# Sparse attention and gated convolution on one core: another division of the DMA issues, fp32 bounds for six pairs, and the order planned again

## The chip, the cores and the metric

The kernel runs on one core of a Trainium2 chip. Five engines work side by side, each through its own list of instructions in order: TensorE (PE in the rows), VectorE (DVE), ScalarE (ACT), GpSimd (POOL) and SyncE (SP), which here only issues DMAs. The metric is the device time of one execution in microseconds; the median of several runs is compared.

## The reference

For 4 batches of 8 heads (768 rows, head size 64) each query may look at 6 of the 24 chunks of 32 keys. Chunks are chosen by an upper bound of the score:

```
k_min, k_max = min and max of k over each chunk
ub   = sum(max(q * k_min, q * k_max)) over the head dimension   # causal chunks only
top  = the 6 chunks with the largest ub
attn = softmax(0.125 * q @ k.T, masked to top and causal)
x    = attn @ v, heads side by side                             # [4, 768, 512]
gate = sigmoid(causal depthwise conv of x, 5 taps)
out  = (gate * (x @ w_val)) @ w_out
```

## The kernel before

The work is cut into 16 pairs of heads, four to a batch. For a pair p the kernel issues small operations, named as the planner names them (name, pair, part):

- **Lk, Lq, Lv** load k, q and v from memory (line 914 for k and q, two DMAs each, line 910 for v) into three buffers of each kind. **KT, QT** transpose k and q on TensorE (line 923), **KE, QH** evict them on ScalarE as fp16 (lines 930 and 966), and **KX** takes the chunk maxima and minima on VectorE (line 936).
- **KB** (lines 946 to 961) and **QL, RL, RH** (lines 974 to 985) split the bounds' operands into a high and a low fp16 part, and **BD** (line 1002) forms the upper bounds with 30 matmuls of 48 columns.
- **MB, T8, CM** (lines 1005 to 1019) add the causal fill `cfill`, take the largest eight and make the mask NS. **MD** (line 1034) transposes NS into QM by DMA; for the pairs not in the set `dmam` **MT and ME** do it on TensorE and VectorE.
- **S** (lines 1046 to 1051) makes the scores in six blocks of two PSUM banks each, the mask being one more matmul of QM with the constant EM. **E** (line 1055) takes the exponential on ScalarE, **A** (line 1067) cuts the causal triangle on GpSimd, and **AV, RC, NR** (lines 1076 to 1087) sum the values and normalize into ON.
- **XT** (line 1105) transposes ON into xT by DMA for the pairs in `dmat`, and **XS** (lines 1111 and 1114) copies halves of it. **CV** (lines 1149 to 1155) is the convolution as 40 matmuls on a quarter of the array each, **TH** (line 1159) its gate on ScalarE.
- When the four pairs of a batch are done, **VL** (line 1166) multiplies by w_val, **GV** gates it on VectorE, **OU** (line 1179) multiplies by w_out, **OE** evicts and **ST** (line 1193) stores.

The order is not written by hand. `schedule` is a list planner: it knows each operation's cost on its engine, picks the ready operation with the lowest priority number that can start soonest, and hands out the eight PSUM banks. The priorities come from the table PARAMS (a period per pair, an offset per kind, an offset per kind and pair). The instructions are then emitted in the planned order, and each engine keeps to it. The planner counts a DMA that ScalarE issues as 100 ns of ScalarE, and one that SyncE issues as 60 ns of SyncE.

Constants (`ident`, `cfill`, `identh`, EM, `ident2`, the convolution weights) are loaded on SyncE's queue between the first loads (lines 1207 to 1227); w_val and w_out on GpSimd's. DMAs from SyncE and ScalarE use eight completion semaphores in turn, so that the ninth waits for the first to land.

Of the kernel before, what the change touches and what calls it, by code (L numbers as in the profile page):

```python
# [10 lines left out]
FP = mybir.dt.float32  # L11
# [63 lines left out]
MODE = 90.0  # L75
XLAT = {"PE": 37, "ACT": 60, "DVE": 57, "POOL": 60, "SP": 60}


def schedule(graph, nbanks=8, quota=None, slack=0.0):
# [15 lines left out]
    dma_free = [0.0, 0.0]  # L95
# [3 lines left out]
    while len(order) < n:  # L99
        best = None  # L100
        for e in engs:
# [5 lines left out]
            tried = 0  # L107
            for pri, i in sorted(r):
# [9 lines left out]
                new = [g for g in o.groups if g.bank is None]  # L118
                if new:
# [5 lines left out]
                    av = sorted(bank_free[b] for b in range(nbanks) if not bank_open[b])  # L125
                    if len(av) < len(new):
                        continue
                    if av[len(new) - 1] > est:
                        est = av[len(new) - 1]
                if cand is None or est < cand[0] - slack:  # L130
                    cand = (est, pri, i)
# [5 lines left out]
            if cand is not None and (best is None or cand < best):  # L137
# [3 lines left out]
        est, pri, i = best  # L141
# [3 lines left out]
        for g in o.groups:  # L145
            if g.bank is None:
                b = min((bank_free[b], b) for b in range(nbanks) if not bank_open[b])[1]
# [4 lines left out]
        if o.dma:  # L152
            q = o.eng == "ACT"
            dma_free[q] = max(dma_free[q], est + 700.0) + o.dma * (1.5 if q else 1.0)
            o.fin = dma_free[q] + 1300.0
            if q:
                dma_free[0] += o.dma
# [15 lines left out]
        for sidx in o.succs:  # L173
# [14 lines left out]
PARAMS = {'T': 11966.2,  # L188
 'off': {'Lk': -41636,
         'Lq': -33293,  # L190
         'Lv': 48651,
         'Lw': -20469,
         'Lc': -37356,
         'Ld': 61141,
         'KT': -17145,
         'KE': -135276,
         'KX': -10835,
         'KB': -27580,
         'QT': -12221,
         'QH': -36726,  # L200
         'QL': -53332,
         'RH': -896,
         'RL': -6554,
         'VC': 15582,
         'BD': -13273,
         'MB': -57904,
         'T8': -43761,
         'CM': -237738,
         'MT': -84078,
         'ME': -110955,  # L210
         'S': -3769,
         'E': 380,
         'A': 4500,
         'AV': 5996,
         'NR': 7483,
         'XT': 29413,
         'XS': 129182,
         'XE': 31813,
         'CV': 28979,
         'TH': 93088,  # L220
         'VL': 38301,
         'VLz': -27255,
         'GV': 27368,
         'OU': 65453,
         'OUz': -23813},
 'kbeng': ['POOL', 'POOL', 'POOL'],
 'border': [5, 4, 3, 1, 0, 2],
 'sstep': 1157.8,
 'avA': 10953.2,
 'avB': 13593.9,  # L230
 'vstep': 2846.9,
 'ostep': 613.2,
 'dmat': {3, 4, 5, 6, 7, 8, 9, 10, 11, 12, 13, 14, 15},
 'dmam': {4, 5, 6, 7, 8, 10, 12, 13, 14},
 'xeng': {'XT': 'DVE', 'XS': 'ACT'},
 'cvcost': 1650.0,
 'quota': {'s': 8, 'av': 2, 'w': 8},
 'slack': 100.0,
 'dl': {('VC', 1): 9000,
        ('RH', 4): -1736,  # L240
        ('Lv', 14): -6295,
        ('OUz', 4): 378,
        ('TH', 13): -13394,
        ('XE', 0): -5226,
        ('E', 14): -4155,
        ('KT', 4): -16168,
        ('TH', 1): 32754,
        ('KT', 6): -1203,
        ('XS', 7): 10081,
        ('KE', 8): -46,  # L250
        ('MT', 14): -14186,
        ('RH', 3): -5716,
        ('E', 4): -17454,
        ('T8', 2): 10374,
        ('Lc', 3): 5791,
        ('RH', 6): -1437,
        ('CM', 2): 15061,
        ('QT', 2): 7714,
        ('CM', 7): -6969,
        ('NR', 3): -2699,  # L260
        ('QT', 5): -214,
        ('KE', 4): 14340,
        ('CV', 4): -2772,
        ('ME', 10): 731,
        ('NR', 4): 3599,
        ('QH', 14): -8614,
        ('VC', 13): -2339,
        ('KX', 13): 578,
        ('XT', 10): -3543,
        ('OUz', 13): -7327,  # L270
        ('VL', 8): -982,
        ('T8', 13): 11117,
        ('KB', 5): -383,
        ('XE', 14): 10692,
        ('MT', 11): -2513,
        ('E', 2): 635,
        ('QL', 3): -3942,
        ('RH', 1): -6652,
        ('RL', 9): 685,
        ('AV', 13): -2326,  # L280
        ('KE', 0): 4923,
        ('AV', 2): -1335,
        ('RH', 2): -954,
        ('VLz', 12): 5318,
        ('CV', 9): -10708,
        ('KT', 9): 46,
        ('Ld', 3): 3582,
        ('S', 14): -5473,
        ('MB', 2): -20083,
        ('KB', 4): 7639,  # L290
        ('T8', 9): 1891,
        ('KB', 2): 2873,
        ('MT', 13): -11694,
        ('VL', 3): -357,
        ('Lw', 8): -483,
        ('QT', 0): -1113,
        ('GV', 13): 2356,
        ('Lk', 14): 22746,
        ('Lq', 15): -20461,
        ('QT', 11): -349,  # L300
        ('OU', 6): -1209,
        ('Lk', 13): -7175,
        ('RH', 0): 20291,
        ('AV', 4): -632,
        ('QL', 1): 18148,
        ('Lk', 10): -568,
        ('KX', 5): -403,
        ('A', 4): 6402,
        ('OU', 14): 5538,
        ('S', 6): -408,  # L310
        ('E', 1): -921,
        ('Lw', 14): 21861,
        ('XE', 10): 3312,
        ('BD', 13): 1202,
        ('A', 13): -3892,
        ('Ld', 13): 19053,
        ('KT', 3): -2737,
        ('KE', 2): 32991,
# [992 lines left out]
```

## Time and profile before

| | us |
|---|---|
| median of 3 runs | 223.14 (222.56 to 225.15) |
| the profiled execution, its own time | 221.15 |
| its span, first to last instruction | 219.4 |
| TensorE busy in the span | 187.2 (85%) |
| VectorE, ScalarE, GpSimd busy | 142.3, 141.4, 95.3 |

Busy time leaves out instructions that issue DMAs. A TensorE record lasts until the modelled end of its matmul, so a row of matmuls overlaps itself.

### The profile page before, as it was taken

The page shows a single profiled execution, that of the slowest core. Times are in us where ns is not written, and L with a number is a line of the kernel's source. Part 1 is how long each engine was busy: PE and PEld are TensorE (multiplying, and loading weights), DVE is VectorE, ACT ScalarE, POOL GpSimd, SP SyncE. Part 2 cuts the span into 40 slices and gives each one's busy share as a digit, 9 for nine tenths or more (in the row PEclk, how much of TensorE's full clock was granted, in tenths as well). Part 3 has the DMA queues.
Part 4 walks back from the last instruction along what each step waited for, and adds up shares of the span by engine and source line. Part 5 has one row for each costly group of instructions (what it writes and reads, how often), then busy time and mean ns, then how long its engine had stood idle before and what let it go on. Part 6 is the DMA issues. An engine that isn't in the chain of part 4 may idle for free.

```text
span 219.4 us, 7282 instructions
## 1 busy us (share of the span) xinstructions
PE 187.2 (85%) x2854; PEld 122.2 (56%) x2854; DVE 142.3 (65%) x458; ACT 141.4 (64%) x313; POOL 95.3 (43%) x237
## 2 busy tenths in 40 slices
PE   1147878989899878898999996989998999999992
PEld 1025555757767555565564683556565666765540
DVE  0419988599885988575671798857576488252332
ACT  3013667979778866686696942877977686925241
POOL 6206499977456635351613521553723633500000
PEclk9999699999999999999999999999999999999998
DMA  5999999983996999439939999901347150139035
GB/s 99 197 198 231 220 201 224 213 186 76 185 211 126 235 169 198 92 71 152 153 105 208 288 187 222 127 23 40 27 143 231 24 69 18 39 57 292 22 118 217
DMA packets 98893, 32.32 MB, mean 147 GB/s; under 512 B 92796, under 2 KB 95788, under 8 KB 98860
## 3 DMA queue, kind: packets, MB, share of 16 engines
q1 hardware_dynamic: 79276, 25.50, 56.1%
q10 hardware_dynamic: 18528, 5.32, 16.5%
q0 software_dynamic: 1056, 1.05, 3.1%
q8 instruction: 22, 0.36, 0.7%
q14 instruction: 11, 0.09, 0.2%
HBM read 21.30 MB, written 6.29 MB: 126 GB/s over the span
## 4 chain that ended last, share of the span: by engine, by line
PE 54%; DVE 15%; DMA 10%; ACT 8%; SPq 4%; issue 3%; POOL 2%; ACTq 2%; DVEq 0%
PE ps L1179 10%; PE ps L1166 7%; PE ps L1149 7%; PE ps L1076 6%; PE ps L1048 5%; PE ps L923 5%; ACT P L1055 5%; PE ps L1051 5%; PE ps L1002 4%; DMA QM<-NS 3%; DMA identh<-identh 3%; SPq L914 3%; PE ps L1151 3%; DVE KK L936 2%; DMA xS<-xT 2%
## 5 line engine op out<-in xcount | busy, mean ns | idle before, releaser
L1055 ACT ACTIVATE P<-ps 128x512 f16<-128x512 f32 (+1 forms) x192 | 89.8, 575 | 18.2 <-PE ps L1051 13.1
L1067 POOL TENSOR_SCALAR_AFFINE_SELECT P<-P 128x128 f16<-128x128 f16 (+1 forms) x128 | 48.3, 393 | 39.7 <-ACT P L1055 37.3
L936 DVE TENSOR_REDUCE KK<-ps 128x12 f32<-128x384 f32 x64 | 32.7, 550 | 13.0 <-ACT KE L930 8.3
L1051 PE MATMUL ps<-QM,EM 64*128 64x512 f16 (+4 forms) x256 | 37.9, 295 | 1.5 <-DVE QM L1032 0.8
L1048 PE MATMUL ps<-QH,KE 64*128 64x512 f16 (+4 forms) x256 | 35.3, 297 | 1.0 <-ACT OSB L1187 0.4
L1151 PE MATMUL ps<-xS,diag 64*64 64x384 f16 x160 | 29.0, 324 | 2.3 <-DVE ON L1087 1.6
L1149 PE MATMUL ps<-xT,diag 64*64 64x384 f16 x160 | 29.4, 325 | 0.0
L1076 PE MATMUL ps<-VA,P 128*128 128x65 f16 x672 | 27.6, 194 | 1.9 <-POOL P L1067 1.1
L1076 PEld LDWEIGHTS <-P 128*128 128x128 f16 x672 | 25.1, 98 | 7.4 <-issue 3.5
L1153 PE MATMUL ps<-xS,diag 64*64 64x384 f16 x160 | 29.0, 325 | 0.0
L1155 PE MATMUL ps<-xT,diag 64*64 64x384 f16 x160 | 29.0, 325 | 0.0
L1159 ACT ACTIVATE G<-ps 128x384 f32<-128x384 f32 x32 | 14.9, 508 | 20.3 <-PE ps L1155 14.3
L974 DVE SCALAR_TENSOR_TENSOR QL<-ps,QH 128x256 f16<-128x256 f32 (+1 forms) x32 | 15.0, 487 | 18.2 <-ACT QH L966 18.0
L1171 DVE SCALAR_TENSOR_TENSOR GV<-G,ps 128x384 f16<-128x384 f32 x32 | 17.4, 548 | 13.8 <-ACT G L1159 7.5
L1166 PE MATMUL ps<-xT,wval 128*128 128x384 f16 x128 | 24.6, 326 | 0.7 <-ACT G L1159 0.5
L989 POOL CAST VA<-vn 128x768 f16<-128x768 f32 x16 | 13.5, 850 | 23.2 <-PE ps L1076 21.7
L966 ACT ACTIVATE QH<-ps 128x384 f16<-128x384 f32 x32 | 15.1, 508 | 12.1 <-PE ps L923 10.3
L923 PE MATMUL ps<-ident,qn 128*128 128x128 f32 x96 | 16.5, 302 | 7.5 <-DMA qn<-in_q_dram 7.3
L1179 PE MATMUL ps<-wout,GV 128*128 128x512 f16 x96 | 22.4, 379 | 0.0
L930 ACT ACTIVATE KE<-ps 128x384 f16<-128x384 f32 x32 | 15.3, 520 | 10.7 <-PE ps L923 7.8
L923 PE MATMUL ps<-ident,kn 128*128 128x128 f32 x96 | 15.7, 298 | 7.3 <-DMA kn<-in_k_dram 5.2
L1149 PEld LDWEIGHTS <-diag 64*64 64x64 f16 x160 | 15.8, 106 | 9.4 <-issue 4.7
(58 smaller groups left out, 365.6 us busy)
## 6 DMA issues: line engine op xcount, KB each, us to landing
vn<-in_v_dram SPq DMA_DIRECT2D x16, 384.0 KB, 5.8
out_dram<-OSB SPq DMA_DIRECT2D x24, 256.0 KB, 2.7
kn<-in_k_dram SPq DMA_DIRECT2D x30, 192.0 KB, 4.6
qn<-in_q_dram SPq DMA_DIRECT2D x30, 192.0 KB, 4.5
xS<-xT ACTq DMA_DIRECT2D x13, 48.5 KB, 2.2
xS<-xT ACTq DMA_DIRECT2D x13, 48.0 KB, 2.7
wval<-in_moe_w_val_dram POOLq DMA_DIRECT2D x1, 512.0 KB, 6.9
wout<-in_moe_w_out_dram POOLq DMA_DIRECT2D x1, 512.0 KB, 9.3
```

Of the source, the lines that this page charges most:

```text
L923: nc.tensor.transpose(out=pt[:, tl * 128:(tl + 1) * 128], in_=t[:, 3 * w + tl, :], identity=ident)
L936: nc.vector.tensor_reduce(out=KK[p % 2][:, mx, w * 12:(w + 1) * 12], in_=bank(gr, None).rearrange("p (c t) -> p c t", t=CH), axis=AX.X, op ...
L1048: nc.tensor.matmul(out=pq[hh][:, col + a:col + n], lhsT=KE[p % 3][HP[hh], ks], rhs=QH[p % 3][HP[hh], q0 + a:q0 + n], start=True, stop=False)
L1051: nc.tensor.matmul(out=pq[hh][:, col + a:col + n], lhsT=EM[HP[hh], ks], rhs=qm[HP[hh], q0 + a - 128:q0 + n - 128], start=False, stop=True)
L1055: e.EX = lambda p, hh, bi, tot, gr: nc.scalar.activation(out=PT[hh, bi, p % 2][:, 0:tot], in_=bank(gr, None)[:, 0:tot], func=AF.Exp, scale ...
L1067: nc.gpsimd.affine_select(out=ap, in_=ap, pattern=[[0, n], [1, 128]], compare_op=ALU.is_ge, fill=0.0, base=0, channel_multiplier=-1)
L1076: nc.tensor.matmul(out=pav[:, qt, :], lhsT=PT[a, bi, p % 2][:, col:col + 128], rhs=VA[p % 3][:, hh, jt, :], start=(jt == 0), stop=(jt == qt))
L1149: nc.tensor.matmul(out=b0[0:64], lhsT=diag[0:64, ct, 0, j, :], rhs=x[0:64, LD - 4 + ki:LD - 4 + ki + HB], start=st, stop=sp)
L1151: nc.tensor.matmul(out=b1[0:64], lhsT=diag[64:128, ct, 0, j, :], rhs=xs[64:128, a:a + HB], start=st, stop=sp)
L1153: nc.tensor.matmul(out=b0[64:128], lhsT=diag[0:64, ct, 1, j, :], rhs=xs[0:64, LD - 4 + ki:LD - 4 + ki + HB], start=st, stop=sp)
L1166: nc.tensor.matmul(out=pv, lhsT=wval_sb[:, ct, et * 128:(et + 1) * 128], rhs=xT[:, s0 + ct, LD + w * HB:LD + (w + 1) * HB], start=(ct == 0 ...
L1179: nc.tensor.matmul(out=po, lhsT=GVT[(b % 2) * NCT + et][:, s * 128:(s + 1) * 128], rhs=wout_sb[:, et, :], start=(et == 0), stop=(et == NCT ...
```

## The change

- The DMA transposes MD and XT and the copies XS go from ScalarE's queue to SyncE's. The first load of q and `ident` go to ScalarE's queue; all other constants go to GpSimd's.
- For the pairs 0, 1, 2, 3, 5 and 11 (`f32`) the bounds are formed in fp32. QL, RL, RH, KB and BD fall away. In their place ScalarE evicts q and relu(q) as fp32 (QF and RF, two pieces each, line 1088), VectorE makes four small tiles KF (lines 1075 and 1077), and BF takes 10 fp32 matmuls of 48 columns (line 1096).
- For the last batch a value sum VL may be split: the first three of its four matmuls as soon as their pairs are transposed, the fourth when the last pair is.
- The planner gets other costs (1240 ns of SyncE for a transpose, 480 for a copy, 800 for a load of k or q), one line of DMA time for all queues, a rule that holds a DMA back while more than 4 us are queued, and a rule that keeps banks for an operation that needs two. PARAMS is new throughout: the score blocks come in the order 3, 0, 1, 4, 2, 5, only one AV bank is open at a time, and the sets are `dmat` = 1 and 4 to 15, `dmam` = 5 to 15.

```diff
+DEEP = 4000.0
+AHEAD = 1000.0
...
+                if o.dma and dma_free - DEEP > est:
+                    est = dma_free - DEEP
...
+                    take = av[held:held + len(new)]
+                    if len(take) < len(new):
+                        if est <= f + AHEAD:
+                            held += len(new)
                         continue
...
-            q = o.eng == "ACT"
-            dma_free[q] = max(dma_free[q], est + 700.0) + o.dma * (1.5 if q else 1.0)
+            dma_free = max(dma_free, est + 700.0) + o.dma
...
- 'border': [5, 4, 3, 1, 0, 2],
+ 'border': [3, 0, 1, 4, 2, 5],
- 'quota': {'s': 8, 'av': 2, 'w': 8},
+ 'quota': {'s': 6, 'av': 1, 'w': 8, 'v': 2},
+ 'lq': {('q', 0): 'ACT'},
+ 'f32': {0, 1, 2, 3, 5, 11},
...
+            if full:
+                g.op("ACT", c, l, f"QF{p}.{w}", lambda w=w, gr=gr: e.QFv(p, w, gr, 0),
+                     [("qps", p, w)], [("QF", k2, w)], [gr], pri(p, "QL", w))
...
+                g.op("PE", 2 * 112, 112 + 285, f"BF{p}.{it}", lambda it=it, gr=gr: e.BF(p, it, gr),
...
-            g.op("ACT", 100, 100, f"MD{p}", lambda: e.MD(p), [("NS", k2)], [("QM", k3)], (),
+            g.op("SP", 1240, 1240, f"MD{p}", lambda: e.MD(p), [("NS", k2)], [("QM", k3)], (),
                  pri(p, "MT"), dma=1050.0)
...
-            g.op("ACT", 100, 100, f"XT{p}", lambda: e.XTd(p), on, [("xT", slot)], (), pri(p, "XT"),
+            g.op("SP", 1240, 1240, f"XT{p}", lambda: e.XTd(p), on, [("xT", slot)], (), pri(p, "XT"),
...
+                    cuts = ((0, NCT),) if not last else ((0, NCT - 1), (NCT - 1, NCT))
...
+    def BF(p, it, gr):
+        pu = bank(gr, [128, SELT, 2 * NCH])
+        ts = slice((it - 1) * 128, it * 128)
+        for n in range(2):
+            nc.tensor.matmul(out=pu[:, it - 1, :], lhsT=QF[p % 2][:, 1 - n, ts],
+                             rhs=KF[p % 2][:, n, :], start=(n == 0), stop=(n == 1))
...
-        sp("cfill", lambda: nc.sync.dma_start(out=cfill, in_=cfill_dr.ap()), [("cfill",)], c0,
+        sp("cfill", lambda en: en.dma_start(out=cfill, in_=cfill_dr.ap()), [("cfill",)], c0,
            400.0)
```

What this moves is seen on SyncE first. Its list before begins so (kn and qn are the buffers of k and q; the first three kn and qn numbers are pairs 0, 1 and 2):

```order
L1207 DMA ident<-identc 128x128
L914 DMA kn_74<-in_k_dram 128x3x64 x4
L1217 DMA cfill<-cfill 128x240
L1219 DMA identh<-identh 128x128
L1223 DMA EM<-echunk 24x768 x2
L1225 DMA ident_63<-ident 128x64
L914 DMA qn_77<-in_q_dram 128x3x64 x4
L914 DMA kn_75<-in_k_dram 128x6x64 x2
```

Now it begins with the loads alone:

```order
L1014 DMA kn_74<-in_k_dram 128x3x64 x4
L1014 DMA kn_75<-in_k_dram 128x6x64 x2
L1014 DMA qn_78<-in_q_dram 128x6x64 x2
L1014 DMA qn_79<-in_q_dram 128x6x64 x2
L1014 DMA kn_76<-in_k_dram 128x6x64 x2
```

And ScalarE's list, which before began with the load of its table and the eviction of k, now begins with two loads:

```order
L1339 DMA ident<-identc 128x128
L1014 DMA qn_77<-in_q_dram 128x3x64 x4
L1088 ACT_TABLE_LOAD
L1088 ACTIVATE QF_104<-ps_199 128x256
L1066 ACTIVATE QH_93<-ps_199 128x384
L1088 ACTIVATE QF_104<-ps_199 128x256
L1030 ACTIVATE KE_83<-ps_194 128x384
```

The five constants stood ahead of q of pair 0 in one queue; they are now in GpSimd's list, behind its seven memsets. The second place is ScalarE in the middle, around the exponentials of pair 4 before the change, where two transposes stand among the activations:

```order
L1055 ACTIVATE P_0_114<-ps_1394 128x512
L1034 DMA_TRANSPOSE QM_88<-NS_113 128x5x128
L1055 ACTIVATE P_0_120<-ps_1395 128x512
L1055 ACTIVATE P_0_116<-ps_1407 128x512
L1055 ACTIVATE P_0_122<-ps_1408 128x512
L1159 ACTIVATE G_144<-ps_1421 128x384
L966 ACTIVATE QH_93<-ps_1480 128x384
L966 ACTIVATE QH_93<-ps_1486 128x384
L1105 DMA_TRANSPOSE xT<-ON_141 128x6x128
L1159 ACTIVATE G_144<-ps_1422 128x384
```

Now such transposes stand on SyncE among the loads, here those of the masks of pairs 5 and 6, of ON of pair 4 and of the mask of pair 7:

```order
L1014 DMA qn_77<-in_q_dram 128x6x64 x2
L1164 DMA_TRANSPOSE QM_88<-NS_117 128x5x128
L1010 DMA vn_81<-in_v_dram 128x12x64
L1164 DMA_TRANSPOSE QM_86<-NS_116 128x5x128
L1014 DMA kn_76<-in_k_dram 128x6x64 x2
L1010 DMA vn_82<-in_v_dram 128x12x64
L1014 DMA qn_78<-in_q_dram 128x6x64 x2
L1010 DMA vn_80<-in_v_dram 128x12x64
L1235 DMA_TRANSPOSE xT<-ON_144 128x6x128
L1164 DMA_TRANSPOSE QM_87<-NS_117 128x5x128
```

ScalarE issues no DMA after its first five; SyncE's list grows from 80 rows to 123, and a transpose there stands behind the loads ahead of it, each of which waits for its buffer to be read.

## Rows read from the trace of the kernel before

**Rows 1.** The page, part 1: engine, busy us (share of the span), instructions.

```profile
PE 187.2 (85%) x2854; PEld 122.2 (56%) x2854; DVE 142.3 (65%) x458; ACT 141.4 (64%) x313; POOL 95.3 (43%) x237
```

**Rows 2.** Stretches: length, busy PE, PEld, DVE, ACT, POOL; granted clock, DMA share, GB/s.

```profile
24.00:72.00 48.00, 43.62 (x771) 31.25 (x766) 39.48 (x131) 39.09 (x90) 35.49 (x83) 0.97 0.94 182
72.00:120.00 48.00, 43.15 (x661) 26.82 (x657) 32.56 (x107) 34.16 (x78) 20.64 (x54) 1.00 0.87 153
120.00:168.00 48.00, 43.97 (x675) 28.60 (x672) 34.99 (x113) 34.65 (x78) 19.80 (x50) 1.00 0.79 140
168.00:190.20 22.20, 21.80 (x400) 14.45 (x400) 13.94 (x49) 17.60 (x42) 11.17 (x29) 1.00 0.28 54
190.20:219.40 29.20, 25.25 (x294) 14.11 (x292) 10.36 (x21) 10.09 (x21) 0.06 (x1) 0.98 0.42 133
```

**Rows 3.** Timeline of the start: start us, us, engine, line, operation [idle before <-releaser].

```profile
5.75 3.97 SPq L914 DMA_DIRECT2D qn<-in_q_dram  x4
...
13.57 1.80 PE L923 MATMUL ps<-ident,qn 128*128 128x128 f32 x6 [7.25 <-DMA qn<-in_q_dram]
...
23.61 0.25 PE L1048 MATMUL ps<-QH,KE 64*128 64x128 f16 x2
```

**Rows 4.** ScalarE's issues by line: ns min/median/max; last row: L1034, issue to landing.

```profile
L1105 ACTq DMA_TRANSPOSE xT<-ON x13: 1227/1232/1810, 69.7 to 196.4; - x13
...
L1034 ACTq DMA_TRANSPOSE QM<-NS x9: 1214/1235/1567, 56.0 to 174.2; - x9
...
L1111 ACTq DMA_DIRECT2D xS<-xT x13: 469/490/1350, 82.9 to 200.5; - x13
...
DMA to landing us min/median/max: 2.6/3.4/6.7
```

**Rows 5.** ScalarE near the end, in order of time.

```profile
196.33 0.60 ACT L1187 ACTIVATE OSB<-ps 128x512 f32<-128x512 f32 x1 [3.81 <-PE ps L1179]
196.41 1.23 ACTq L1105 DMA_TRANSPOSE xT<-ON  x1
```

**Rows 6.** The page, part 2: GB/s moved in 40 equal slices of 5.5 us.

```profile
GB/s 99 197 198 231 220 201 224 213 186 76 185 211 126 235 169 198 92 71 152 153 105 208 288 187 222 127 23 40 27 143 231 24 69 18 39 57 292 22 118 217
```

**Rows 7.** DMA issues of the whole run: KB each, median us from issue to landing.

```profile
kn<-in_k_dram SPq DMA_DIRECT2D x30, 192.0 KB, 4.6
...
xS<-xT ACTq DMA_DIRECT2D x13, 48.0 KB, 2.7
...
xT<-ON ACTq DMA_TRANSPOSE x13, 4.1
```

**Rows 8.** Groups of instructions by shape: count, busy us, mean ns.

```profile
L966 ACT ACTIVATE QH<-ps 128x384 f16<-128x384 f32 x32 | 15.1, 508 | 12.1 <-PE ps L923 10.3 <-DVE GV L1171 1.6
...
L985 DVE SCALAR_TENSOR_TENSOR RL<-QH,QL 128x640 f16<-128x640 f16 x16 | 14.9, 928 | 0.1
...
L974 DVE SCALAR_TENSOR_TENSOR QL<-ps,QH 128x384 f16<-128x384 f32 x16 | 8.8, 553 | 1.5 <-ACT QH L966 1.4
...
L953 DVE SCALAR_TENSOR_TENSOR KC<-KK,KC 128x48 f16<-128x48 f32 x16 | 4.7, 292 | 4.4 <-POOL KC L950 4.2
```

**Rows 9.** Pieces of the chain of waits: start us, us, engine, line, instructions.

```profile
144.09 0.91 PE ps L1002 x30
...
160.09 0.69 PE ps L923 x6
...
192.97 1.33 PE ps L1076 x42
194.31 4.32 PE ps L1179 x20
...
200.38 2.71 PE ps L1166 x16
...
206.24 0.28 PE ps L1149
...
208.00 1.41 PE ps L1166 x8
```

More of the change, by code (lines that the diff above doesn't have):

```diff
@@ L118, in schedule @@
                 new = [g for g in o.groups if g.bank is None]
+                take = ()
                 if new:
@@ L136, in schedule @@
                     break
-            if cand is not None and (best is None or cand < best):
+            if cand is not None and (best is None or cand[:3] < best[:3]):
                 best = cand
@@ L140, in schedule @@
             raise RuntimeError("stuck: " + " ".join(ops[i].name for e in engs for _, i in ready[e][:9]))
-        est, pri, i = best
+        est, pri, i, take = best
         o = ops[i]
@@ L146, in schedule @@
             if g.bank is None:
-                b = min((bank_free[b], b) for b in range(nbanks) if not bank_open[b])[1]
+                b = take.pop(0)
                 g.bank = b
@@ L186, in schedule @@
     return order, max(o.fin for o in ops)
[L188 to L225, printed above, removed]
- 'kbeng': ['POOL', 'POOL', 'POOL'],
- 'border': [5, 4, 3, 1, 0, 2],
[L228 to L234, printed above, removed]
+PARAMS = {'T': 7973.0,
+ 'off': {'Lk': -42705,
+         'Lq': -33893,
+         'Lv': -22368,
+         'Lw': 4896,
+         'Lc': -78769,
+         'Ld': 37114,
+         'KT': -17058,
+         'KE': 100677,
+         'KX': -22340,
+         'KB': -72087,
+         'QT': -13788,
+         'QH': -12929,
+         'QL': 40671,
+         'RH': 64641,
+         'RL': -251142,
+         'VC': 36468,
+         'BD': -10821,
+         'MB': -169501,
+         'T8': 98434,
+         'CM': 138908,
+         'MT': -16966,
+         'ME': -140244,
+         'S': 636,
+         'E': 76167,
+         'A': -26629,
+         'AV': -776,
+         'NR': -129785,
+         'XT': 6011,
+         'XS': -146314,
+         'XE': -26156,
+         'CV': -36237,
+         'TH': -26668,
+         'VLa': 161748,
+         'VL': 16447,
+         'VLz': -16701,
+         'GV': -48370,
+         'OU': 36292,
+         'OUz': 221795},
+ 'kbeng': ['POOL', 'POOL', 'POOL'],
+ 'border': [3, 0, 1, 4, 2, 5],
+ 'sstep': 953.1,
+ 'avA': 10954.4,
+ 'avB': 7795.0,
+ 'vstep': 1421.7,
+ 'ostep': 2568.9,
+ 'dmat': {1, 4, 5, 6, 7, 8, 9, 10, 11, 12, 13, 14, 15},
+ 'dmam': {5, 6, 7, 8, 9, 10, 11, 12, 13, 14, 15},
@@ L549, in mm @@
+ 'lq': {('q', 0): 'ACT'},
+ 'f32': {0, 1, 2, 3, 5, 11},
+ 'rqeng': 'ACT'}
 def mm(n):
@@ L903, with load @@
     cq = {"k": (kn, k), "q": (qn, q), "v": (vn, v)}
-    def load(what, p, part, nsp):
+    def load(what, p, part, nsp, eng):
+        en = nc.sync if eng == "SP" else nc.scalar
         t, src = cq[what]
@@ L969, with KFb, QFv @@
     e.QHv = QHv
+    def KFb(p, hh, n):
+        kk = KK[p % 2]
+        o = KF[p % 2][HP[hh], n, CC[hh] * NCH:(CC[hh] + 1) * NCH]
+        if n == 0:
+            nc.vector.tensor_tensor(out=o, in0=kk[HP[hh], 0], in1=kk[HP[hh], 1], op=ALU.subtract)
+        else:
+            nc.vector.tensor_copy(out=o, in_=kk[HP[hh], 1])
+    e.KFb = KFb
+    def QFv(p, w, gr, relu):
+        a = 128 if w == 0 else 0
+        o = QF[p % 2][:, 1 if relu else 0, w * HB + a - 128:(w + 1) * HB - 128]
+        src = bank(gr, None)[:, a:HB]
+        if relu == "DVE":
+            nc.vector.tensor_scalar(out=o, in0=src, scalar1=0.0, scalar2=None, op0=ALU.max)
+        else:
+            nc.scalar.activation(out=o, in_=src, func=AF.Relu if relu else AF.Copy)
+    e.QFv = QFv
+    def BF(p, it, gr):
+        pu = bank(gr, [128, SELT, 2 * NCH])
+        ts = slice((it - 1) * 128, it * 128)
+        for n in range(2):
+            nc.tensor.matmul(out=pu[:, it - 1, :], lhsT=QF[p % 2][:, 1 - n, ts],
+                             rhs=KF[p % 2][:, n, :], start=(n == 0), stop=(n == 1))
+    e.BF = BF
     def QLv(p, w, gr):
@@ L1206, in setup_graph @@
         e0 = -1.0e6
-        sp("ident", lambda: nc.sync.dma_start(out=ident, in_=ident_dr.ap()), [("ident",)], e0,
-           220.0)
+        sp("ident", lambda en: en.dma_start(out=ident, in_=ident_dr.ap()), [("ident",)], e0,
+           220.0, "ACT")
         for i in range(2):
+            ms("DVE", f"mKF{i}", KF[i], 0.0, [("KF", i, hh, n) for hh in range(2) for n in range(2)],
+               e0 + 20 + i, 120)
             ms("POOL", f"mKB{i}", KB[i], 0.0, [("KB", i, 0), ("KB", i, 1)], e0 + i)
```

822 lines of the change are left out of this document (452 added, 370 removed).

## The prediction

> **What bounds the kernel now.** I read the page's busy times first, then the stretches, then the timeline of the start and the chain of waits at the end.
>
> TensorE is the busiest engine, 187.2 of 219.4 us [rows 1]. The stretches show that this is not one state but three [rows 2]. From 24 to 190.2 us TensorE is busy 43.62 + 43.15 + 43.97 + 21.80 = 152.5 of 166.2 us, so 13.7 us are idle there. In the last stretch it is busy 25.25 of 29.2 us, and what is missing is the eviction and the store of the last rows after its last matmul. The first 24 us are a wait. The transposes of q of pair 0 could not start before 13.57 us: their four loads were issued only between 5.75 and 9.72 us, because five DMAs of constants stood ahead of them on the same queue and because each DMA must wait for the one eight places before it. So the first score matmul stands at 23.61 us [rows 3].
>
> ScalarE looks free with 141.4 us [rows 1], but the page does not count what its queue does. It issues 13 transposes XT of 1.232 us, 9 transposes MD of 1.235 us and 26 copies XS of at least 0.49 us: 16.0 + 11.1 + 12.7 = 39.8 us, all between 56 and 201 us [rows 4]. With the 135.6 us of activations in 24 to 219.4 us, which are the sum of the ACT column [rows 2], that is 175 us of 195, as much as TensorE has there (177.8). Not all of it holds the activations up, since an issue may begin while an activation still runs. One place shows that it can: an eviction stands idle 3.81 us and begins at 196.33 us, and 0.08 us later the queue takes up the next transpose for 1.23 us [rows 5]. The eviction's matmuls, one fifth of 4.32 us from 194.31 us on, ended near 195.2 us [rows 9], so about 1.1 of the 3.81 us were not the matmuls' doing. The next eviction waits for a bank's matmul no longer than for that transpose. Scores need banks that ScalarE empties, so a late ScalarE is how part of TensorE's 13.7 us comes about.
>
> **The change part by part**, against the profiled execution's 221.15 us (span 219.4).
>
> *Start.* Loads of q for pair 0 go out on ScalarE's queue at the same time as those of k on SyncE's, without a constant ahead. What then sets the first score is either the chain of operations or the bytes. By the chain: nothing of q is needed before about 5 us, where before it was 13.57 us [rows 3], and the operations between the two rows took 10.0 us; they do not get shorter on ScalarE, which now makes four evictions more for the pair. That gives 15 us. By the bytes: TensorE's list has the transposes of k and q of pairs 0 to 2 ahead of the first score, which is 12 DMAs' worth of 192 KB, 2.36 million bytes [rows 7], and the constants add some 0.3 million by their shapes. At the rates of the first three slices, 99, 197 and 198 GB/s over 5.5 us each, 2.71 million bytes are there after 16.5 us [rows 6]. I take 16.6 us, the later of the two: **7.0 us less**. The ends: 15 us (8.6 less), and 20 us (3.6 less) if `cfill`, now behind seven memsets and on GpSimd's queue, comes late; it is the last thing needed for the first mask.
>
> *The middle, ScalarE freed.* The 39.8 us leave ScalarE. The fp32 pairs give some back: four evictions each, at most 0.508 us each [rows 8], 2.0 us per pair and 12 us for six, of which about half falls before the first score. So ScalarE's load between first score and end falls from 175 to some 142 us and it is no longer level with TensorE. This gain has no row of its own. Below it is bounded by nothing at all, above by the 13.7 us of idle TensorE. I take 9, two thirds: the idle time is spread over the whole stretch in small pieces, as a chain score, exponential, triangle, value sum makes it, and ScalarE was the only other engine as full. **9.0 us less.**
>
> *The fp32 bounds on TensorE.* Thirty fp16 matmuls took 0.91 us, so a fp32 form is cheaper only if its 10 matmuls take under 0.09 us each. No fp32 matmul that is not a transpose of that size is in the trace. The nearest is the fp32 transpose of 128 columns, six in 0.69 us or 0.115 us each [rows 9]: ten make 1.15 us, 0.24 us more per pair, and **1.4 us more** for six. The lower end is the fp16 price of 0.03 us, 3.7 us less in all; the upper end, twice the transpose, costs 8.3 us. On VectorE the pair loses RL (0.928) and QL (0.553 for the larger half) and more, and gains four small tiles of at most 0.292 us as KC [rows 8], so at least 0.3 us is saved; VectorE is not the bound (39.48 of 48 us at most, [rows 2]) and I set it at nothing.
>
> *The end.* From 190.2 us to its last matmul TensorE never stops, so starting value sums earlier within that stretch saves nothing by itself; it fills the wait for the last convolution. Before, that convolution began at 206.24 us, 11.9 us after the last attention sum (192.97 + 1.33 us). In the new order the work between the two is one OU block (0.86), 19 VL matmuls of 2.71/16 us (3.2) and two convolutions of 1.76 us (206.24 to 208.00), 7.6 us in all [rows 9]. The data takes: normalizing, about 0.9 us; the transpose to landing 4.1 us; the first copy's issue 0.5 us, and the second copy's landing 2.7 us [rows 4, 7], 8.2 us. So TensorE waits some **0.6 us**; nothing if the transpose is quick, 3 us if it lands as late as the latest mask did (6.7 against 3.4, [rows 4]).
>
> *SyncE.* It takes 24 transposes and 26 copies, 24 x 1.23 + 26 x 0.5 = 43 us of issuing, beside 104 loads and stores, which at the same 0.5 us make 52 us. That is 95 us of some 205 and I set it at nothing. The cover is the prefetch: three buffers of each of q, k and v, so a load may be late by a pair. Without it the mask's transposes, which stand among these loads, would pay (third rival).
>
> Sum: -7.0 - 9.0 + 1.4 + 0.6 = **-14.0 us**. On the profiled execution that is 207.2 us, on the median of the runs shown, which stands 2.0 us higher, 209.1. I say **207.5**.
>
> **The rivals.**
>
> *More is won (chance 0.20).* Busy TensorE is not full TensorE: sixteen VL matmuls back to back take 2.71 us, 0.17 each [rows 9]; a stall shorter than a matmul's way through the array shows as busy time. If the new order also removes these, and the start reaches 15 us, the gain is 8.6 + 13.7 and a few us more: 197 to 203. For it: ScalarE had no slack. Against it: VectorE stays as it was, and some of these stalls are its own.
>
> *Only the start is won (0.16).* The middle keeps its pace because it hangs on VectorE's chain to the mask or on the DMA engines, whose share is 0.94 and 0.87 in the first two stretches [rows 2]; the loads are not fewer, and time taken from the start presses them together. Then -7.0 + 1.4 + 0.6 = -5.0: 216 to 218.
>
> *Slower: the masks wait in one queue (0.07).* Before, the transposes had ScalarE's queue to themselves and landed in 3.4 us in the median, 2.6 at best and 6.7 at worst [rows 4]. Now each stands in the queue of the loads. A load of 384 KB of v or a pair of 192 KB takes about 2 us at 200 GB/s [rows 6], and several may be ahead. Each of the 11 masks of pairs 5 to 15 releases its pair's scores. If each arrives 2 us after the other work has run out, TensorE stops for 22 us: 229. It decides from 11 x 1.5 us on, where 14 us of gain and the 2.2 us of a measurable loss are used up. Against it: all that nine such masks cost TensorE before lies within its 13.7 idle us, and a mask can be formed while the previous pair's scores run. The Trainium skill ("DMA: Bandwidth & Descriptors", section "Queues, rings and completion order") speaks for this rival: each DMA engine takes turns between the queues that have work, but keeps the order within one. By that rule a transpose that used to take turns with the loads now follows all that are ahead. The trace shows no transpose on the loads' queue, so it neither bears the rule out nor denies it.
>
> *No change (0.07).* The five fp32 pairs among the first six load ScalarE where it is already at 39.09 of 48 us [rows 2]; 2 us for each eats the start's 7 us, and the middle gives nothing: 221 to 225.
>
> **How the numbers follow.** My forecast, 204 to 212, has 0.50. A difference of 1% (2.2 us) is about what runs of this kernel can tell from none. The first two rivals are faster too: 0.50 + 0.20 + 0.16 = 0.86 faster, 0.07 the same, 0.07 slower. The range 196 to 219 takes in the forecast and the first two rivals but for their edges, about 0.82.
>
> **What would show it.** Right: the first score matmul near 16.6 us; no issue rows on ScalarE after the first; TensorE idle under 6 us from first score to last; 10 fp32 matmuls in about 1.15 us; a gap of under 1 us before the last convolution. Wrong: masks that land in over 6 us with TensorE idle behind them (third rival); a first score after 20 us; the same idle time in the middle with ScalarE now idle too (second rival).

## The result, and the profile after

The changed kernel takes **213.43 us** (median of 4 runs, 213.03 to 220.26) against 223.11 us of the kernel before on the same chip: ratio 0.9544, 95% interval 0.9467 to 0.9621, some 9.7 us faster. The forecast was 207.5 us with a range of 196 to 219. The profiled execution took 213.03 us with a span of 211.3 us, against 221.15 and 219.4 us: 8.1 us between the two traces, 1.6 us less than between the medians, because the profiled execution of the kernel before lies under its median. A run far above the quickest of its kernel, such as the one of 220.26 us (mean granted clock 0.961, against 0.984 for the others) or one of 272.73 us further down (0.649), counts in medians and ranges and not in ratios.

The page of the changed kernel, part 1 and two rows of part 2 (slices of 5.3 us); they answer to [rows 1] and [rows 6]:

```profile
PE 195.6 (93%) x2784; PEld 134.5 (64%) x2784; DVE 130.8 (62%) x452; ACT 149.2 (71%) x337; POOL 89.7 (42%) x220
...
PEclk9999799999978999999999999999999999999999
...
GB/s 151 229 218 218 213 117 225 54 225 139 174 227 84 85 223 175 191 209 182 171 248 260 213 147 160 186 101 108 108 28 161 121 54 2 40 158 231 47 71 226
```

TensorE has 70 instructions fewer and is busy 8.4 us longer, in a span that is 8.1 us shorter.

Where the time went is read from two stretches, from the first score to the last, and from there to the end (columns as in [rows 2]):

```profile
23.30:183.80 160.50, 156.53 (x2463) 107.79 (x2463) 112.84 (x396) 129.98 (x295) 82.62 (x199) 0.99 0.80 149
183.80:211.30 27.50, 22.74 (x242) 12.51 (x242) 8.31 (x17) 9.81 (x21) 1.45 (x5) 1.00 0.49 143
```

The first score comes 0.3 us sooner, the stretch of scores is 6.1 us shorter (23.6 to 190.2 us before, 166.6 us), and the rest 1.7 us (29.2 us before, [rows 2]). In the stretch of scores TensorE stands idle for 4.0 us, where it was 13.7; 3.6 us of that gain are lost again to work that it now does more.

The start, TensorE's timeline of the changed kernel (columns as in [rows 3]):

```profile
5.59 0.87 PE L1023 MATMUL ps<-ident,qn 128*128 128x128 f32 x3 [0.33 <-DMA qn<-in_q_dram]
...
8.98 4.48 PE L1096 MATMUL ps<-KF,QF 128*128 128x48 f32 x20 [0.30 <-DVE KF L1077]
13.25 1.51 PE L1023 MATMUL ps<-ident,kn 128*128 128x128 f32 x6
...
17.86 1.06 PE L1096 MATMUL ps<-KF,QF 128*128 128x48 f32 x8 [1.19 <-DVE KF L1077]
19.14 0.45 PE L1158 MATMUL ps<-identh,NS 128*128 128x128 f16 x5 [0.22 <-DVE NS L1149]
19.43 2.03 PE L1096 MATMUL ps<-KF,QF 128*128 128x48 f32 x12
21.27 0.87 PE L1023 MATMUL ps<-ident,qn 128*128 128x128 f32 x3
21.93 1.49 PE L1023 MATMUL ps<-ident,kn 128*128 128x128 f32 x6
23.34 0.24 PE L1176 MATMUL ps<-QH,KE 64*128 64x64 f16 x2
```

q of pair 0 is transposed at 5.59 us, 8.0 us sooner than in [rows 3]. The place of q in its queue is not the only reason. In the kernel before, GpSimd loads w_val (and w_out at 3.44 us) ahead of the first scores, and from 4 to 12 us its queue, q0, moves 1.04 MB and SyncE's, q1, 0.46 MB (MB, share of the 16 engines' time):

```profile
2.46 0.98 POOL L1231 DMA_DIRECT2D wval<-in_moe_w_val_dram  x1
...
q0 software_dynamic: 1045, 1.04, 85.6%
q1 hardware_dynamic: 1367, 0.46, 28.2%
```

In the order of the changed kernel these two loads begin at 39.46 and 50.82 us. No run parts the two causes.

And yet the first score stands at 23.34 us. In between are the fp32 bounds, and they have 20 instructions, not 10: 4.48 us for pair 0, 224 ns each, and 3.09 us for pair 1. VectorE, at the same time:

```profile
14.16 1.72 DVE L1036 TENSOR_REDUCE KK<-ps 128x12 f32<-128x384 f32 x3 [5.24 <-PE ps L1023]
15.91 0.41 DVE L1135 TENSOR_TENSOR MUB<-ps,cfill 128x240 f32<-128x240 f32 x1
```

It stood idle for 5.24 us. The bounds of pair 0 were ready near 13.45 us, but the chunk maxima of pair 1 stand ahead of its mask in VectorE's list, and the mask begins at 15.91 us. It is transposed at 19.14 us, and TensorE waits only 0.22 us for it; but then the rest of pair 1's bounds and nine more transposes of q and k stand ahead of the first score. The time is TensorE's own list. From q's first transpose to the first score it is busy for 15.55 of 17.75 us; in the kernel before it was 7.29 of 10.04 us (columns as in [rows 2], the changed kernel first):

```profile
5.59:23.34 17.75, 15.55 (x78) 13.64 (x78) 8.70 (x36) 8.21 (x22) 0.83 (x1) 0.91 1.36 222
...
13.57:23.61 10.04, 7.29 (x61) 5.62 (x62) 7.83 (x29) 3.17 (x7) 3.46 (x5) 1.00 1.19 207
```

The bounds take 7.57 us of it (two pairs in fp32), where they took 1.41 us (one pair in fp16); 33 transposes take 8.09 us, where 24 took 5.71. Three kernels further down with the same operations ahead of the first score show the first score at 24.49, 24.75 and 24.92 us, so the 0.3 us gained here are within what executions differ by.

Away from the start the same bounds are twice as quick, here on the chain of waits (start us, us, engine, line, instructions), with six transposes in place of the 1.51 us above:

```profile
119.11 2.17 PE ps L1096 x20
...
128.47 0.69 PE ps L1023 x6
```

That is 108 ns against 224, and 0.115 us a transpose against 0.25: until about 17 us TensorE works at half the rate, as 1.2 is to 2.4 GHz, although the granted clock reads 1.00 there. The eight bounds at 17.86 us take 132 ns each, and from about 20.5 us on the transposes are back at 0.25 us; there the clock reads 0.50:

```profile
8.98:13.46 4.48, 4.48 (x21) 4.48 (x22) 0.00 (x0) 1.37 (x4) 0.00 (x0) 1.00 1.38 218
...
20.50:23.00 2.50, 2.50 (x14) 2.50 (x13) 0.98 (x6) 0.77 (x3) 0.00 (x0) 0.50 1.39 221
```

The transposes of the masks, now on SyncE (ns min/median/max of the issue, first and last start; then issue to landing):

```profile
L1164 SPq DMA_TRANSPOSE QM<-NS x11: 1201/1507/2378, 69.2 to 171.3; - x11
...
DMA to landing us min/median/max: 2.6/3.7/4.8
```

Behind the loads they land in 2.6 to 4.8 us; alone on ScalarE's queue it was 2.6 to 6.7 [rows 4].

### The profile page after: what moved, and what is told of

Same layout as the page of the kernel before. It is cut to its first block, busy times and chain, and to the rows that moved or that the text cites. A ratio compares the mean times of both kernels' runs of the same rounds, so it can differ in the third digit from the quotient of the medians.

```text
span 211.3 us, 7144 instructions
## 1 busy us (share of the span) xinstructions
PE 195.6 (93%) x2784; PEld 134.5 (64%) x2784; DVE 130.8 (62%) x452; ACT 149.2 (71%) x337; POOL 89.7 (42%) x220
## 4 chain that ended last, share of the span: by engine, by line
PE 73%; DVE 11%; DMA 8%; ACT 5%; issue 1%; ACTq 0%; SPq 0%; DVEq 0%
PE ps L1309 9%; PE ps L1296 9%; PE ps L1023 8%; PE ps L1279 8%; PE ps L1206 8%; PE ps L1096 7%; PE ps L1178 7%; PE ps L1181 6%; DMA xT<-ON 4%; PE ps L1132 3%; DVE KK L1036 3%; ACT P L1185 2%; PE ps L1281 2%; DMA qn<-in_q_dram 2%; PE ps L1176 2%; DMA out_dram<-OSB 1%
## 5 line engine op out<-in xcount | busy, mean ns | idle before, releaser
L1185 ACT ACTIVATE P<-ps 128x512 f16<-128x512 f32 x192 | 89.8, 585 | 11.9 <-PE ps L1181 11.5
L1197 POOL TENSOR_SCALAR_AFFINE_SELECT P<-P 128x256 f16<-128x256 f16 (+1 forms) x128 | 47.2, 379 | 62.5 <-ACT P L1185 59.7
L1181 PE MATMUL ps<-QM,EM 64*128 64x512 f16 (+4 forms) x256 | 36.7, 290 | 0.0
L1206 PEld LDWEIGHTS <-P 128*128 128x128 f16 x672 | 26.5, 98 | 6.2 <-issue 1.8
L1206 PE MATMUL ps<-VA,P 128*128 128x65 f16 x672 | 29.0, 194 | 0.2 <-ACT P L1185 0.2
L1309 PE MATMUL ps<-wout,GV 128*128 128x512 f16 x96 | 23.6, 379 | 0.0
L1289 ACT ACTIVATE G<-ps 128x384 f32<-128x384 f32 x32 | 13.9, 488 | 13.5 <-PE ps L1285 13.3
L1119 POOL CAST VA<-vn 128x768 f16<-128x768 f32 x16 | 13.3, 837 | 18.1 <-DMA vn<-in_v_dram 11.2
L1096 PE MATMUL ps<-KF,QF 128*128 128x48 f32 x120 | 17.9, 309 | 2.2 <-DVE KF L1077 1.7
L1096 PEld LDWEIGHTS ps<-KF,QF 128*128 128x128 f32 x120 | 17.1, 224 | 3.8 <-ACT QF L1088 1.6
L1178 PEld LDWEIGHTS <-KE 64*128 64x128 f16 x256 | 12.8, 94 | 9.8 <-issue 4.5
```

What stands on the lines that cost most here:

```text
L1096: nc.tensor.matmul(out=pu[:, it - 1, :], lhsT=QF[p % 2][:, 1 - n, ts], rhs=KF[p % 2][:, n, :], start=(n == 0), stop=(n == 1))
L1178: nc.tensor.matmul(out=pq[hh][:, col + a:col + n], lhsT=KE[p % 3][HP[hh], ks], rhs=QH[p % 3][HP[hh], q0 + a:q0 + n], start=True, stop=False)
L1181: nc.tensor.matmul(out=pq[hh][:, col + a:col + n], lhsT=EM[HP[hh], ks], rhs=qm[HP[hh], q0 + a - 128:q0 + n - 128], start=False, stop=True)
L1185: e.EX = lambda p, hh, bi, tot, gr: nc.scalar.activation(out=PT[hh, bi, p % 2][:, 0:tot], in_=bank(gr, None)[:, 0:tot], func=AF.Exp, scale ...
L1197: nc.gpsimd.affine_select(out=ap, in_=ap, pattern=[[0, n], [1, 128]], compare_op=ALU.is_ge, fill=0.0, base=0, channel_multiplier=-1)
L1206: nc.tensor.matmul(out=pav[:, qt, :], lhsT=PT[a, bi, p % 2][:, col:col + 128], rhs=VA[p % 3][:, hh, jt, :], start=(jt == 0), stop=(jt == qt))
```

## The experiments

Where an edit touches the planner's input (the set of fp32 pairs, the split of the value sums), the order was planned again; in the others it stayed.

### The changed kernel, its transposes and copies issued by ScalarE again

```diff
-    e.MD = lambda p: nc.sync.dma_start_transpose(
+    e.MD = lambda p: nc.scalar.dma_start_transpose(
```

The same edit for XT and both copies XS.

> The changed kernel in its planned order; only the DMA transposes of masks and attention sums and the copies of xT are issued from ScalarE again. Theory 1 (ScalarE's issuing time made TensorE's idle time in the middle): 24 transposes and 26 copies put about 43 us back on ScalarE, which is busy 149 us; TensorE's idle time in the middle returns from 4 to 8 us or more, 218 to 223 us. Rival (the new order, planned with true costs, removed the idle time whoever issues): 212 to 215 us, and TensorE's idle time stays near 4 us.

Measured: 227.88 us, ratio to before 1.0166 (1.0083 to 1.0248). With the order of the changed kernel and only the issuing engine put back, 14.4 us are lost by the medians, more than was expected, and the kernel is no quicker than the one before. The stretch of scores, TensorE's waits (line, what for: us in total, times, longest), and ScalarE's busiest group:

```profile
24.40:197.40 173.00, 161.02 (x2463) 107.88 (x2463) 114.20 (x396) 130.54 (x295) 82.85 (x199) 0.99 0.75 137
```
```profile
PE ps L1178 <- ACT P L1185: 3.1, 6, 0.9
...
PE ps L1023 <- ACT P L1185: 2.1, 2, 1.8
PE ps L1296 <- ACT P L1185: 2.1, 2, 1.4
PE ps L1206 <- ACT P L1185: 0.8, 2, 0.6
```
```profile
L1185 ACT ACTIVATE P<-ps 128x512 f16<-128x512 f32 x192 | 90.7, 578 | 22.9 <-PE ps L1181 14.8 <-DVE KK L1036 2.0 <-PE ps L1132 1.6
```

TensorE is idle for 12.0 us where it was 4.0, and 8.1 us of its waits in the whole run have the exponentials as what came last (1.0 us in the changed kernel). The stretch is 12.5 us longer; the other 4.5 us are in TensorE's busy time, for the same 2463 matmuls, and what makes them is not shown. The exponentials are no longer than before (578 ns), but ScalarE is idle ahead of them for 22.9 us, against this in the changed kernel:

```profile
L1185 ACT ACTIVATE P<-ps 128x512 f16<-128x512 f32 x192 | 89.8, 585 | 11.9 <-PE ps L1181 11.5 <-POOL P L1197 0.2
```

Of those 22.9 us the scores ended the idle time in 14.8. In the chain of waits ScalarE's queue has rows of its own:

```profile
193.24 0.90 ACTq L1235
198.45 1.23 ACTq L1235
```

The second is a whole transpose of 1.23 us that stands in the chain.

### The kernel before, its transposes and copies issued by SyncE

```diff
-    e.XTd = lambda p: nc.scalar.dma_start_transpose(
+    e.XTd = lambda p: nc.sync.dma_start_transpose(
```

The same edit for MD and XS.

> The kernel before in its planned order; only the transposes and copies are issued from SyncE. Theory 1: 39.8 us leave ScalarE, TensorE's 13.7 idle us fall to 6 or less, 214 to 219 us. Rival (order alone): 221 to 225 us. Third (masks wait behind loads in one queue): slower than 225 us, with TensorE waiting for masks that land in over 5 us.

Measured: 217.9 us, ratio 0.9724 (0.9665 to 0.9783). In an order that was planned for the other queue, the move alone gives 6.2 us of the 9.7. The masks (issue to landing), and what TensorE waits for:

```profile
DMA to landing us min/median/max: 2.6/3.5/4.3
```
```profile
PE ps L1151 <- DMA xS<-xT: 4.2, 5, 1.3
PE ps L1051 <- DMA QM<-NS: 3.7, 2, 2.6
```

The waits behind the loads exist here, 7.9 us in sum (1.5 us in the kernel before); in time they come out smaller than what ScalarE gains. In the stretch of scores, 163.85 us instead of 166.6, TensorE's idle time hardly falls:

```profile
23.65:187.50 163.85, 151.38 (x2497) 101.16 (x2496) 120.66 (x400) 126.36 (x285) 86.27 (x215) 0.99 0.80 147
```

It is 12.5 us, where it was 13.7 and 6 or less were expected. The gain is shown by the medians; by way of idle time it is not. The two traces differ by 2.7 us only, since the one of the kernel before lies low among its runs and this one is the highest of its four.

### The kernel before, with the start's loads divided as in the change

```diff
-            nc.sync.dma_start(
+            (nc.scalar if what == "q" and p == 0 else nc.sync).dma_start(
```

`ident` goes to ScalarE's queue as well, and the other constants to GpSimd's, where they stand ahead of w_val: its load begins at 6.99 us instead of 2.46.

> The kernel before in its planned order; only the first load of q and ident go to ScalarE's queue and the other constants to GpSimd's. Theory 3 (the start was held by the place of q behind the constants, and the change lost this gain to the fp32 matmuls): q of pair 0 is transposed by 7 us instead of 13.57, the first score comes at 17 to 20 us instead of 23.6, and 3 to 6 us are won, 217 to 220 us. Rival (the first score is set by bytes, or the time won at the start is given back in the middle): 222 to 225 us.

Measured: 221.39 us, ratio 0.9871 (0.9785 to 0.9957), some 2.9 us less. TensorE's timeline:

```profile
8.52 1.49 PE L923 MATMUL ps<-ident,qn 128*128 128x128 f32 x6
...
20.63 0.29 PE L1048 MATMUL ps<-QH,KE 64*128 64x128 f16 x2
```

q is there 5.0 us sooner, by both causes together, and the first score 3.0 us sooner than in [rows 3]. From there to the end it takes 199.1 us, where it was 195.8, so in the trace the start's gain is given back; by the medians most of it stays. This is not settled.

### The changed kernel, with half of the fp32 matmuls

The second matmul of every sum is left out, so the bounds lack one of their two terms.

```diff
-        for n in range(2):
+        for n in range(1):
...
-                             rhs=KF[p % 2][:, n, :], start=(n == 0), stop=(n == 1))
+                             rhs=KF[p % 2][:, n, :], start=True, stop=True)
```

> The changed kernel in its planned order with the second of the two fp32 matmuls of each bound left out, so that the bounds are not those of the reference. Theory 2 (TensorE is the bound and the fp32 bounds lie on it with 2.17 us a pair, 4.48 us in pair 0): half of the 17.9 us of their rows is gone, 8 us less in the sum, 204 to 208 us, and the first score comes 3 us earlier. Rival (they lie beside waits for VectorE and loads): 211 to 214 us and TensorE's idle time grows instead.

Measured: 205.98 us, ratio 0.9174 (0.911 to 0.9239), 7.4 us under the changed kernel. The first bounds and the first score:

```profile
9.23 2.30 PE L1096 MATMUL ps<-KF,QF 128*128 128x48 f32 x10
...
19.82 0.24 PE L1176 MATMUL ps<-QH,KE 64*128 64x64 f16 x2
```

Half the instructions take half the time, and the first score comes 3.5 us sooner. The fp32 matmuls are on the path that sets it. TensorE is busy 186.3 us instead of 195.6.

The same for the pairs 3, 5 and 11 alone:

> The changed kernel in its planned order; the second fp32 matmul of the bounds is left out for the pairs 3, 5 and 11 alone, so that their masks are not those of the reference. With both halves gone in all six pairs 7.5 us were won. If TensorE is the bound from first score to last, these three pairs give 3 x 1.1 = 3.3 us of it: 209.5 to 211 us. Rival (the gain was the start's, where these matmuls run at half the rate): 212.5 to 213.5 us.

Measured: 212.52 us, ratio 0.9546 (0.9467 to 0.9624), which can't be told from the changed kernel. By difference, what half the matmuls were worth lay in the first three pairs.

### Other sets of fp32 pairs

```diff
- 'f32': {0, 1, 2, 3, 5, 11},
+ 'f32': set(),
```

> The changed kernel with no fp32 pair (all bounds in fp16 parts), planned again with the same table otherwise. Theory 2 (TensorE is the bound and fp32 bounds take 17.9 us of it where fp16 takes 0.9 a pair, 5.4 us): up to 12 us less, 202 to 209 us. Rival (the fp16 way puts 2.6 us of VectorE and over 1 us of GpSimd back on each pair, its mask comes later, and the table was made for the fp32 pairs): 212 to 219 us.

Measured: 224.68 us, ratio 1.0074 (1.0029 to 1.012). Without a fp32 pair the whole gain is gone, although TensorE has less to do for each pair; both the expectation and its rival were lower. The next two sets narrow down where.

Pair 0 alone:

> The changed kernel with fp32 bounds for pair 0 alone, planned again. Theory 2: five pairs less of 1.3 us or more on TensorE, 204 to 209 us. Rival: 212 to 218 us.

Pairs 0, 1 and 2:

> The changed kernel with fp32 bounds for pairs 0, 1 and 2 alone, planned again. Theory 2: pairs 3, 5 and 11 take 1.3 us each less, 208 to 211 us. Rival: 212 to 217 us.

Measured: 223.37 us (1.0017, 0.9983 to 1.005) with pair 0, and 212.21 us (0.9523, 0.9468 to 0.9577) with three. So pairs 1 and 2 carry 11.2 us, and the pairs 3, 5 and 11 nothing that can be measured. Pair 0 alone, its longest wait on TensorE, and the stretch behind the start:

```profile
PE ps L1132 <- POOL KB L1061: 5.3, 2, 3.9
```
```profile
24.00:72.00 48.00, 39.53 (x564) 25.63 (x564) 34.34 (x124) 30.22 (x69) 35.30 (x76) 0.87 0.92 172
```

The set of three, the same stretch:

```profile
24.00:72.00 48.00, 43.17 (x707) 30.37 (x709) 42.26 (x147) 37.97 (x86) 36.59 (x80) 1.00 0.85 158
```

With pair 1 in fp16 its bounds wait for GpSimd's KB; once, for 3.9 us, ahead of the first score. GpSimd stands idle there for 3.3 us until VectorE has KK, and VectorE is full; from 16 to 28 us, pair 0 alone first and then the set of three:

```profile
16.00:28.00 12.00, 6.69 (x96) 5.81 (x97) 11.76 (x45) 2.69 (x6) 4.61 (x11) 0.89 1.30 216
...
16.00:28.00 12.00, 10.94 (x67) 8.63 (x65) 7.91 (x39) 7.34 (x20) 1.68 (x3) 1.00 1.16 186
```

VectorE is busy for 11.76 of 12 us, with the set of three for 7.91; QL, RL and RH of the fp16 form are 6.1 us of it. The mean over 48 us, 34.34 against 42.26 us, hides this. The first score comes at 27.19 us instead of 24.92. These 2.3 us are a part of the 10.5 us between the two traces. In the stretch of scores TensorE is idle for 2.9 us more and, with 2468 instructions instead of 2493, busy for 4.6 us more; its granted clock reads 0.96 of 2.4 GHz there in the mean, 1.00 with the set of three. Over the whole span all ten runs with pair 0 alone have 0.954 to 0.969, the four with the set of three 0.984 to 0.996. How the late start and the lower clock hang together was not tested. The priorities of the table belong to the set of six, so part of the 11.2 us may be an order that does not suit the other sets; a table made for them was not tried.

### The value sums of the last batch unsplit

```diff
-                    cuts = ((0, NCT),) if not last else ((0, NCT - 1), (NCT - 1, NCT))
+                    cuts = ((0, NCT),)
```

> The changed kernel with the last value sums in one piece. The prediction's reading (TensorE never stops at the end, so the pieces only fill the wait for the last convolution): up to 2 us slower, 213.5 to 216 us, with a longer wait of TensorE on the copies of xT. Rival (the pieces take banks or change nothing): 212.5 to 213.5 us.

Measured: 214.29 us, ratio 0.9588 (0.9522 to 0.9653): 0.9 us above the changed kernel, within the intervals. Inconclusive. In the changed kernel TensorE waits here once, for xT of the last pair:

```profile
PE ps L1296 <- DMA xT<-ON: 1.0, 1, 1.0
```

### Matmuls of zeros, so that TensorE has no gaps at the start

```diff
+    wz = ct_([128, 512], F16, "wz")
...
+        nc.vector.memset(wz, 0.0)
+        pw = ps.tile([128, 512], FP, tag="b7", name="ps_warm")
+        def warm(n):
+            for _ in range(n):
+                nc.tensor.matmul(out=pw, lhsT=wz[:, 0:128], rhs=wz, start=True, stop=True)
+        warm(8)
```

> The changed kernel with eight matmuls of zeros of 512 columns on TensorE ahead of everything, in the time when it waits for the first load. Theory 4 (TensorE stands at its lower clock for the first 20 us because it has been idle, and BF of pair 0 takes 4.48 instead of 2.2 us for that alone): with the clock up by 9 us the first score comes 3 to 6 us earlier, 207 to 211 us. Rival (the zeros end too early and the clock stays down, or the first score waits for VectorE and loads): 212.5 to 214.5 us.

Measured: 213.26 us (211.8 to 272.73), ratio 0.9553 (0.9463 to 0.9642): eight matmuls ahead of the list change nothing that can be measured. The trace is of the longest run, so what the first bounds took in the others is not shown. The next kernel adds one behind each of the first four groups of transposes:

```diff
+            if graph.ops[i].name in ("KT0.0", "QT0.0", "KT0.1", "QT0.1"):
+                warm(1)
```

> The same with one more such matmul behind each of the first four transposes, which stand 0.3 to 0.5 us apart. Theory 4: at least as good as eight alone, 207 to 210 us, and BF of pair 0 at 2.2 to 3 us. Rival: 213 to 215 us, since four matmuls of zeros add up to 1.7 us to the path.

Measured: **209.68 us**, ratio 0.941 (0.9332 to 0.9487). TensorE's timeline:

```profile
4.63 0.61 PE L1023 MATMUL ps<-ident,kn 128*128 128x128 f32 x3
...
8.53 2.56 PE L1096 MATMUL ps<-KF,QF 128*128 128x48 f32 x20
...
13.21 0.52 PE L1023 MATMUL ps<-ident,qn 128*128 128x128 f32 x3 [0.80 <-DMA qn<-in_q_dram]
14.51 1.50 PE L1096 MATMUL ps<-KF,QF 128*128 128x48 f32 x8 [0.78 <-DVE KF L1077]
...
16.33 2.74 PE L1096 MATMUL ps<-KF,QF 128*128 128x48 f32 x12
...
20.95 0.24 PE L1176 MATMUL ps<-QH,KE 64*128 64x64 f16 x2
```

The bounds of pair 0 take 2.56 us, 128 ns each, instead of 4.48, and the first score comes 2.4 us sooner; by the medians 3.8 us are gained, with intervals that just overlap. At 16.33 us the matmuls are back at 228 ns, behind gaps of 0.80 and 0.78 us, and the granted clock reads 0.50. The four matmuls without the eight were not tried. The last kernel joins the filling with the set of three:

> The changed kernel with the fp32 bounds in pairs 0, 1 and 2 alone, and with the matmuls of zeros ahead of TensorE's list and after the first four transposes. Theory (two independent gains): the filled gaps take the first score from 24.9 us to about 21 us and the short set keeps its shorter middle (first score to end 186.1 us in the kernel with the fp32 set of three and no filling), so 207 to 208.5 us, ratio 0.93. Rival (TensorE's rate at the start depends on where the gaps of this order lie, and the second set's order has others): BF of pair 0 stays near 4.4 us, first score 23 to 25 us, 211 to 213 us.

Measured: **207.6 us** (206.78 to 209.59), ratio 0.9304 (0.9225 to 0.9384), the quickest whole kernel here, 5.8 us under the changed one, with no overlap of the intervals. Its timeline shows the same:

```profile
8.63 2.40 PE L1096 MATMUL ps<-KF,QF 128*128 128x48 f32 x20
...
20.86 0.24 PE L1176 MATMUL ps<-QH,KE 64*128 64x64 f16 x2
```

The intervals of the last two kernels overlap, so that the shorter set adds to the filling is likely and not shown.

## Why the prediction was right or wrong

**The reading of what bounds the kernel** held in part. That ScalarE's issuing, which the page leaves out, costs time is shown in both orders: put back in the new one it loses 14.4 us, taken away from the kernel before it gives 6.2 us. That it made the idle time of TensorE is shown for the new order alone, where it brings it from 4.0 to 12.0 us. In the kernel before, the move leaves 12.5 of the 13.7 idle us. Neither the move nor the new order by itself, but the two together, bring the idle time down.

**The middle** was forecast at 9.0 us less by idle time falling from 13.7 to about 5 us. The idle time fell to 4.0 us. The stretch got shorter by 6.1 us only, since TensorE is busy 3.6 us more in it; the bounds alone are 5.9 us more there (10.36 us in fp32 and 9.56 in fp16, where all took 14.05).

**The fp32 bounds** are the term that was mis-sized, and the start failed by it. The working took ten matmuls at the time of a fp32 transpose, 1.15 us a pair. Each is two instructions of 108 ns: 2.17 us, near the upper end of "twice the transpose", and 4.48 us at the start. It then charged every pair with it as work beside other work, 1.4 us more in sum; the six pairs' bounds take 17.9 us, and at the fp16 price of 0.91 us they would take 5.5, so 12.4 us more, beyond the upper end of 8.3. For pairs 0 and 1 it is on the path to the first score: halving it took 3.5 us off.

**The start** was forecast at 7.0 us less and gave 0.3. Loading was right to a few tenths: q is transposed at 5.59 us. The step that failed is that the operations between q and the first score would take 10.0 us as before. From 5.59 us on they took 17.75. The trace accounts for the 7.75 us too many by TensorE's work: 6.2 us more for the bounds, because they are in fp32 and because those of pair 1 stand ahead of the first score too, and 2.4 us more for transposes, while its idle time is 0.55 us less and 0.40 us of transposes of the convolution weights are gone from there. Halving the fp32 matmuls took 3.5 us off. That pair 0's mask stands behind the chunk maxima of pair 1 on VectorE cost TensorE a wait of 0.22 us. The working compared bytes with a chain and took the later of the two; a third limit, TensorE's own list at half its rate, is the one that counted. The reading of the start also left out the loads of the weights, 1.04 MB beside q's. The rows for the half rate were there: six transposes take 1.80 us at 13.57 us [rows 3] and 0.69 us later on [rows 9].

**VectorE** was set at nothing, and that was wrong too, in the other direction. The fp32 form takes the splitting of pairs 1 and 2 off VectorE, and the way over GpSimd with it, just ahead of the first score, where VectorE is full without it (11.76 of 12 us); by the sets of pairs 11.2 us hang on it. The working took VectorE for free by its mean over 48 us.

**The end** was forecast at 0.6 us more and is 1.7 us less. No gap stands before the last convolution, the one wait is 1.0 us for xT, and 2.5 us of TensorE's work left the stretch (25.25 to 22.74 us busy).

**The rivals.** "Masks wait in one queue" did not come about: no mask took over 4.8 us. The rule of the Trainium skill ("DMA: Bandwidth & Descriptors", section "Queues, rings and completion order"), by which a DMA engine takes up what stands in one queue in its order, is not contradicted: the loads' queue made TensorE wait 3.7 us for masks in the kernel before with SyncE's issues, and in the changed kernel's order no instruction waited for one, so that the rule's price is a matter of the order. "Only the start is won" came out the other way round: the middle was won and the start was not. "More is won" would have needed both.

**The sum.** Forecast -14.0 us; the traces show -0.3 - 6.1 - 1.7 = -8.1. The 6.7 us missing at the start are more than the whole difference of 5.9. That the time lies in the stated range is in part luck: 213.43 us is neither in the 204 to 212 of the forecast nor in the 216 to 218 of a rival, and the term of the start, 7.0 us, did not come about. The two large parts do not add: with the new table, taking away either the move to SyncE (14.4 us) or the fp32 pairs (11.3 us) loses everything. Which of the planner's rules and numbers make that order work was not tried apart.

## What to carry to other kernels

An engine's issuing of DMAs is work that a page of busy times can leave out; add it to its busy time before calling the engine free, and test it by moving the issues and nothing else. Price an operation at the place where it will stand, by rows of that place: in the first 17 us of this kernel a matmul costs twice what it costs later (224 against 108 ns), and every one that stands ahead of the first score delays all that follows. When a load is brought forward, list what then stands between it and the first useful work on each engine, since that list, not the load, may set the time. And look for a full engine in the stretch just before a wait: a mean over 48 us showed VectorE free where it was full.

## What the runs showed of the hardware that was not expected

- A fp32 matmul of 128x128 by 48 columns is two instructions of 108 ns each, with a weight load of 192 ns in the median for each; it is 7 times the 0.030 us of a fp16 one at 48 columns [rows 9].
- TensorE runs at half its rate for the first 17 us or so (224 against 108 ns a bound) while the granted clock reads 1.00; the durations tell it, the clock row does not. When the half rate comes back at 20.5 us, the clock reads 0.50. Eight matmuls of zeros ahead of the list changed no median; four more in the gaps between the first transposes brought the first bounds from 224 to 128 ns an instruction and 3.8 us off the median of the whole, with intervals that just overlap.
- A DMA transpose costs the issuing queue 1.2 us on SyncE as on ScalarE [rows 4], in the median 1.5 us for the masks and 1.26 us for xT among the loads. On SyncE nothing waits behind it but other DMAs.
